# Seven block products instead of eight for five of the seven down-projection groups of an FFT-mixer and gated-MLP kernel, with products that accumulate on in their PSUM banks

## The chip, the cores and the metric

The kernel runs on one core of a Trainium2 chip. The metric is the device time of one execution in microseconds (us), taken as the median of repeated runs; lower is better. A core has a matrix engine (PE in the profile, with PEld for its weight loads), a vector engine (DVE), a scalar engine (ACT), a general engine (POOL), and SP, which here only issues DMAs. Matmuls write PSUM, of which a partition has eight banks of 512 float32. POOL touches only the on-chip memory SBUF; DVE and ACT read PSUM and SBUF.

## The reference

```python
# x: 1 x 2048 x 640;  w_gate, w_up: 640 x 1728;  w_down: 1728 x 640
def _A_ref(x, w_r, w_i):                      # filter in the 2-D Fourier domain
    X = jnp.fft.rfft2(x, axes=(-2, -1)) * (w_r + 1j * w_i)
    return jnp.fft.irfft2(X, s=(S, D), axes=(-2, -1))
def _B_ref(x, w_gate, w_up, w_down):
    g = jnp.einsum("bsd,df->bsf", x, w_gate)
    u = jnp.einsum("bsd,df->bsf", x, w_up)
    return jnp.einsum("bsf,fd->bsd", g * u, w_down)
h  = x + _A_ref(_layernorm(x), w_r, w_i)
h2 = h + _B_ref(_layernorm(h), w_gate, w_up, w_down)
```

## The kernel before, in words

The first 187 us or so are the Fourier filter, done as matmuls with cosine and sine tables, the second layer norm, and the start of the MLP. The rest is the MLP, and the change lies there.

The 2048 tokens form two blocks (`blk` 0 and 1) of eight tiles of 128 tokens; the first four tiles of a block are its half `sb` 0, the other four its half `sb` 1. The 1728 features form 14 chunks of 128 (the last has 64). Two chunks make a group `p`, whose rows of w_down are loaded together: group 6 (chunks 12 and 13) comes first in each block and is computed plainly, then groups 0 to 5 (chunks 0 to 11). In a group, the chunk `2p` is called even here and `2p+1` odd.

Every float32 operand of a matmul is split into a high part, rounded by ACT to the matmul's format, and a low part, the remainder, computed by DVE or POOL. A product then takes three matmuls: high·high, high·low, low·high.

For one chunk of a block, `strassen` computes gate and up of both halves as a 2x2 block matrix by Strassen's scheme: seven products `o1` to `o7` of 128x512 outputs, 54 matmuls of 512 columns in all, each product in a PSUM bank of its own (tile `e`). DVE adds them up with SBUF tiles `u2`, `u3`, `c22`, `p1` (lines 898 to 925), multiplies gate by up, ACT writes the high part of the result `h` (lines 911, 927) into `ht`, DVE the low part (lines 914, 930). The weights of the next chunk are prepared meanwhile in `prep`: ACT copies the high part of `stage` (the raw weights, a single buffer, filled by DMA in `load_raw`), POOL computes the low part (line 796), four block sums (799 to 802) and their low parts (812).

The down projection of a group runs while the next group's gate and up are computed: `down` takes one tile of 128 tokens, multiplies its `h` of two chunks by w_down (two halves of 320 columns, 12 matmuls in a `pair` of PSUM banks, tile `y`), and `acc` adds the 128x640 result to the residual `X[t]` in SBUF on DVE (line 601). The eight tiles are issued by `some` at fixed places inside `strassen`, all during the even chunk; the odd chunk has no down matmuls. One of the eight is held back at the end of a block (`defer`).

Nothing is reordered: the order of each engine's instructions is the order of the code. Each engine runs its own queue in order and waits on semaphores for others. The pool `work` (tag `wk`) hands out its buffers in turn; an allocation waits until the last reader of its buffer is done.

Of the kernel before, what the change touches and what calls it, by code (L numbers as in the profile page):

```python
# [16 lines left out]
P = 128  # L17
# [4 lines left out]
NC = 14  # L22
# [16 lines left out]
def f32(ap):  # L39
    return ap.bitcast(F32)  # L40
# [29 lines left out]
def tile_spectral_glu(ctx: ExitStack, tc: tile.TileContext, x, wf, wgu, wlast, wdown, wdlast,  # L70
# [4 lines left out]
    work = ctx.enter_context(tc.tile_pool(name="work", bufs=6))  # L75
# [14 lines left out]
    def bank(tag, bufs=2):  # L90
        return pools["y" if tag in ("im2", "ir2") else "a"].tile([P, 512], F32, tag=tag, name=tag, bufs=bufs)
# [4 lines left out]
    def single():  # L96
        return bank("e", 4)

    def wk(shape, name):
        return work.tile(shape, F32, tag="wk", name=name)  # L100
# [464 lines left out]
    def load_d(p):  # L565
        w = home("dA" if p in (0, 2, 4) else "dB", [P, 2, 1280], "wd", F32R)
        return split_in(("d", p), w, wdown[p] if p < 6 else wdlast, [wk([P, D], "draw") for _ in range(2)], nc.gpsimd)
# [106 lines left out]
    def t34(m):  # L674
        src = TJ["b"][:, :, 2 * m:2 * m + 2].rearrange("p j k n -> p k j n")
        hi, lo = ((t3[:, :, l] if m == 0 else xt[:, 1, 0:2, l]).rearrange("p k (j n) -> p k j n", j=4)
                  for l in range(2))
        return [lambda: act(hi, src, AF.Copy), lambda: tt(lo, src, f32(hi), op=OP.subtract)]
# [58 lines left out]
    def gate_parts(c, sb, slot, mid=()):  # L737
        pg, pu = PG[c, sb][0:2]
        u = wk([P, 512], "u")
        hh, hl = hts[:, slot, sb, 0], hts[:, slot, sb, 1]  # L740
# [12 lines left out]
    late = None  # L753
    for t in range(NT):
        for k in tside[t]:
            turn_mm(k)
        if t + 2 < NT:
            unfold(t + 2, dside[t], tside[t])
        else:
            for k in tside[t]:  # L760
                turn_hi(k)
                turn_lo(k)
        if t + 3 < NT:
            id_mm(t + 3)
        for f in aside[t]:
            f()
        if t == NT - 3:
            is1_mm(t)
            ht = home("qm", [P, 8192], "ht", F32R)
            hts, t3 = cut(ht, 0, 3, 2, 2, 512), cut(ht, 6144, 2, 2, 512)  # L770
            banks("a", "pglu")
            gu(NC - 1, 0)
        else:
            is1_mm(t)
        acc(t, PY[t], total[:, t:t + 1] if t < 8 else None)
        if t == NT - 2:
            late = gate_parts(NC - 1, 0, 0)
# [49 lines left out]
    def down(blk, p, slots, j, last=False, defer=False):  # L827
        t = blk * 8 + j
        sb, i = divmod(j, 4)
        ps = pair("y")  # L830
        w = W["d", p].rearrange("p l (c d) -> p l c d", c=2)
        seq = []
        for ci in range(2):
            hh, hl = (hts[:, slots[ci], sb, l, i * P:(i + 1) * P] for l in range(2))
            seq += [(hh, w[:, 0, ci]), (hh, w[:, 1, ci])]
            if 2 * p + ci < NC - 1:
                seq.append((hl, w[:, 0, ci]))

        def half(o, b):
            for n, (l, r) in enumerate(seq):  # L840
                mmx(o, l, r[:, 320 * b:320 * b + 320], n == 0, n == len(seq) - 1)

        if last and blk == 1 and j == 7:
            for b in range(2):
                o = (ps if b == 0 else pair("y"))[:, 0, 0:320]
                xv, ov = X[t][:, 320 * b:320 * b + 320], rows(out, t)[:, 320 * b:320 * b + 320]
                half(o, b)
                tt(xv, o, xv, op=OP.add)
                (nc.sync, nc.scalar)[b].dma_start(ov, xv)
            return  # L850
        for n, (l, r) in enumerate(seq):
            for b in range(2):
                mmx(ps[:, b, 0:320], l, r[:, 320 * b:320 * b + 320], n == 0, n == len(seq) - 1)
        if defer:
            return lambda: acc(t, ps)
        acc(t, ps)
        if last:
            nc.sync.dma_start(rows(out, t), X[t])

# [5 lines left out]
    def strassen(c, blk, slot, ahead, downs, side):  # L865
        wa, ws = W[c]

        def some(n):
            for _ in range(n):
                if downs:  # L870
                    downs.pop(0)()
                    if c:
                        pop(1)

        def at(n):
            for f in side.get(n, ()):
                f()
# [5 lines left out]
        hh, hl = ([hts[:, slot, sb, l] for sb in range(2)] for l in range(2))  # L883

        def product(w, a, ms, extra=()):
            o = single()
            triple(o, [(w, a + P * i, m) for i, m in enumerate(ms)] + list(extra))
            return o

        o1 = product(wa, 384, b11)  # L890
        p1, u2 = wk([P, 512], "p1"), wk([P, 512], "u2")
        act(p1, o1, AF.Copy)
        o6 = product(ws, 0, t2)
        at(0)
# [3 lines left out]
        tt(u2, o6, p1, op=OP.add)  # L898
        at(1)
        o7 = product(ws, 640, [(t3[:, k, 0], t3[:, k, 1]) for k in range(2)])  # L900
        u3, c22 = wk([P, 512], "u3"), wk([P, 512], "c22")
        tt(u3, u2, o7, op=OP.subtract)
        o5 = product(ws, 256, t1, [(wa, 896, b5[1])])
        tt(u2, o5, u2, op=OP.add)  # L904
        tt(c22, o5, u3, op=OP.add)
        some(2)
        at(2)
        o3 = product(ws, 896, b22, [(ws, 512, b5[1])])
        tt(o3, o3, u2, op=OP.add)  # L909
        tt(o3, o3, c22, op=OP.mult)  # L910
        act(hh[1], o3, AF.Copy)  # L911
        at(3)
        some(1)
        tt(hl[1], o3, f32(hh[1]), op=OP.subtract)
        some(1)
        o2 = product(wa, 0, b21, [(wa, 256, b5[0])])
        if ahead:
            ahead[2]()
            ahead[3]()
        tt(p1, o2, p1, op=OP.add)  # L920
        o4 = product(wa, 640, t4, [(wa, 896, b5[0])])
        some(1)
        at(6)
        tt(o4, o4, u3, op=OP.add)
        tt(o4, o4, p1, op=OP.mult)  # L925
        at(7)
        act(hh[0], o4, AF.Copy)  # L927
        at(4)
        some(2)
        tt(hl[0], o4, f32(hh[0]), op=OP.subtract)  # L930
        some(8)
        at(5)
# [3 lines left out]
    count = 0  # L936
    prev = None
    for n, (blk, p) in enumerate(steps):
        if p == 6:
            s13, s12 = count % 3, (count + 1) % 3  # L940
            if blk == 0:
# [14 lines left out]
                late = gate_parts(NC - 2, 0, s12)  # L956
# [4 lines left out]
                late = gate_parts(NC - 1, 1, s13)  # L961
# [8 lines left out]
            else:  # L970
# [17 lines left out]
                down(*prev, js[7], True)  # L988
                gu(NC - 1, 0)
                gate_parts(NC - 1, 0, s13)()  # L990
# [3 lines left out]
                late = gate_parts(NC - 2, 0, s12)  # L994
# [4 lines left out]
                gu(NC - 1, 1)  # L999
                for j in range(4):  # L1000
                    t1s[j][1]()
                wdn = load_d(p)
                late = gate_parts(NC - 1, 1, s13)
# [5 lines left out]
            gate_parts(NC - 2, 1, s12, wdn[0] if blk == 0 else ())()  # L1009
            for f in t34(1):  # L1010
                f()
            issue(wdn, (0, 1) if blk else (1,))
            prev = (blk, 6, (s12, s13))
            count += 2
# [4 lines left out]
            continue  # L1019
        wdn = load_d(p)  # L1020
        downs = [lambda j=j, prev=prev: down(*prev, j) for j in range(8)]
        slots = (count % 3, (count + 1) % 3)
        held = []
        if p == 5:
            downs.pop(3)
        for ci in range(2):
            c = 2 * p + ci
            side = {}
            ahead = None
            if c < 11:  # L1030
                ahead = prep(c + 1, blk)
                side[5] = [lambda c=c: load_raw(c + 2)] if c < 10 else []
            if ci == 0:
                side[3] = [lambda wdn=wdn: issue(wdn)]
            if c == 11 and blk == 0:
                pop(len(fill))
                dj = load_direct(1, [wk([P, D], "draw"), stage[:, 0:640], stage[:, 640:1280]])
                side[1] = [lambda: issue(dj[0]), lambda: issue(dj[1]), lambda: load_raw(0)]
# [7 lines left out]
                side[2] = [lambda: low(range(8))]  # L1046
            if c == 11:
                side[6] = [lambda prev=prev: held.append(down(*prev, 3, defer=True))]
                if blk == 0:
                    side[6] = [lambda: turn_mm(8)] + side[6] + [lambda: turn_hi(8)]  # L1050
                side[7] = [lambda: held[0]()]
            strassen(c, blk, slots[ci], ahead, downs if ci == 0 else [], side)
            count += 1
        prev = (blk, p, slots)
# [133 lines left out]
```

## Time and profile before

| what | value |
|---|---|
| time, median of 3 runs | 707.08 us (706.98 to 707.14) |
| profiled execution: first to last instruction (span) | 705.1 us |
| PE busy | 695.0 us, 3904 instructions |
| DVE busy | 459.3 us |
| ACT busy | 256.4 us |
| POOL busy | 281.6 us |
| granted clock of PE | 1.000 |
| bytes moved by DMA | 55.06 MB, mean 78 GB/s |

Busy times of the engines overlap. The profiled execution is one run of the same program; its span stands 1.98 us below the median of the timed runs, which also hold what lies before its first and behind its last instruction. A line of the profile such as `L106 PE MATMUL y<-wd,ht` names the code line, engine, operation, the tile written and the tiles read. Line 106 is the helper `mmx`, through which nearly all matmuls go, so groups are told apart by their tiles: `e<-...,wst` is gate and up, `y<-wd,ht` the down projection.

### The profile page before, as it was taken

To read this page: it belongs to the slowest core of one execution; us is meant where nothing else is said; L and a number is where in the kernel's file an instruction comes from. 1 tells how busy PE (TensorE), PEld (TensorE's weight loads), DVE (VectorE), ACT (ScalarE), POOL (GpSimd) and SP (SyncE) were. 2 spreads that over 40 slices of the span, in tenths; PEclk is the share of its full clock that TensorE was granted. 3 is DMA by queue.
4 is the path that set the end of the run, shared out by engine and by line. 5 is a ranking of instruction groups with operands and counts; after the bars stand their busy time and mean duration, and the time that the engine had idled before them with its cause. 6 is when DMAs were issued, how large, how long until landed. Compare 5 with 4: busy or idle time off the path is not lost.

```text
span 705.1 us, 10121 instructions
## 1 busy us (share of the span) xinstructions
PE 695.0 (99%) x3904; PEld 619.7 (88%) x3904; DVE 459.3 (65%) x807; ACT 256.4 (36%) x497; POOL 281.6 (40%) x260
## 2 busy tenths in 40 slices
PE   8999999999999999999999999999999999999998
PEld 8989998887798988888898989888888989898987
DVE  7968886998865566565655557565545555555464
ACT  6976664485522222131222273442212222322210
POOL 3101114321264645454535524074545454464600
PEclk9999999999999999999999999999999999999999
DMA  9426762001310102121212113301212121210103
GB/s 334 185 80 197 231 216 87 1 1 39 112 38 31 53 29 75 38 76 37 75 39 75 56 39 150 112 0 38 75 38 75 39 75 38 74 39 11 64 1 150
DMA packets 21073, 55.06 MB, mean 78 GB/s; under 512 B 2336, under 2 KB 7200, under 8 KB 21024
## 3 DMA queue, kind: packets, MB, share of 16 engines
q1 hardware_dynamic: 20304, 52.53, 21.4%
q0 software_dynamic: 288, 1.48, 0.6%
q8 instruction: 31, 0.51, 0.3%
q10 hardware_dynamic: 432, 0.39, 0.2%
q14 instruction: 18, 0.15, 0.1%
HBM read 49.16 MB, written 5.24 MB: 77 GB/s over the span
## 4 chain that ended last, share of the span: by engine, by line
PE 87%; DVE 7%; DMA 2%; issue 1%; ACT 1%; POOL 1%; SPq 0%; ACTq 0%; DVEq 0%
PE e L106 47%; PE y L106 26%; PE re L106 2%; PE im L106 2%; PE u L410 2%; DMA x<-in_x_dram 2%; PE im L452 2%; PE eo L106 2%; PE im L238 1%; PE ir L452 1%; DVE x L601 1%; DVE x L603 1%; DVE q L586 1%; DVE xt L648 1%; DVE q L587 1%
## 5 line engine op out<-in xcount | busy, mean ns | idle before, releaser
L106 PE MATMUL e<-xt,wst 128*128 128x512 f32 x864 | 206.8, 390 | 0.0
L106 PE MATMUL y<-wd,ht 128*128 128x320 f32 x1312 | 201.5, 310 | 0.6 <-DVE x L601 0.5
L106 PEld LDWEIGHTS y<-wd,ht 128*128 128x128 f32 x1312 | 195.3, 188 | 4.8 <-DVE x L601 1.7
L106 PEld LDWEIGHTS e<-xt,wst 128*128 128x128 f32 x864 | 160.7, 188 | 31.7
L601 DVE TENSOR_TENSOR x<-y,x 128x640 f32<-128x640 f32 x119 | 97.7, 822 | 69.9 <-PE y L106 69.4
L796 POOL TENSOR_TENSOR wst<-raw,wst 128x1024 fp32r<-128x1024 f32 x23 | 55.6, 2416 | 153.5 <-ACT wst L795 138.9
L812 POOL TENSOR_TENSOR wst<-raw,wst 128x896 fp32r<-128x896 f32 (+1 forms) x46 | 65.0, 1436 | 22.3 <-ACT wst L807 22.3
L557 POOL TENSOR_TENSOR wd<-draw,wd 128x640 fp32r<-128x640 f32 x28 | 44.9, 1629 | 71.8 <-ACT wd L556 71.8
L106 PE MATMUL e<-t,wst 128*128 128x512 f32 x288 | 73.2, 389 | 0.0
L911 ACT ACTIVATE ht<-e 128x512 fp32r<-128x512 f32 x24 | 14.4, 599 | 154.0 <-DVE e L910 154.0
L106 PEld LDWEIGHTS e<-t,wst 128*128 128x128 f32 x288 | 54.0, 188 | 11.7 <-DVE ht L747 0.5
L927 ACT ACTIVATE ht<-e 128x512 fp32r<-128x512 f32 x24 | 14.4, 599 | 111.8 <-DVE e L925 108.0
L106 PE MATMUL e<-xt,wdir 128*128 128x512 f32 x180 | 42.1, 393 | 0.2 <-DVE ht L751 0.2
L106 PEld LDWEIGHTS e<-xt,wdir 128*128 128x128 f32 x180 | 33.5, 188 | 7.6 <-issue 0.6
L795 ACT ACTIVATE wst<-raw 128x1024 fp32r<-128x1024 f32 x24 | 25.4, 1057 | 31.1 <-DMA raw<-in_wgu_dram 31.1
L106 PE MATMUL e<-ht,wst 128*128 128x512 f32 x144 | 36.5, 389 | 0.0
L904 DVE TENSOR_TENSOR u<-e,u 128x512 f32<-128x512 f32 x24 | 16.6, 692 | 29.5 <-PE e L106 29.4
L481 POOL CAST qr<-bits 1x128 fp32r<-1x128 f32 x15 | 4.2, 282 | 71.3 <-DVE qr L485 71.3
L106 PEld LDWEIGHTS e<-ht,wst 128*128 128x128 f32 x144 | 27.0, 188 | 5.6
L898 DVE TENSOR_TENSOR u<-e,p 128x512 f32<-128x512 f32 x24 | 16.6, 691 | 22.6 <-PE e L106 22.1
L909 DVE TENSOR_TENSOR e<-e,u 128x512 f32<-128x512 f32 x24 | 16.8, 700 | 22.0 <-PE e L106 22.0
L807 ACT ACTIVATE wst<-raw 128x896 fp32r<-128x896 f32 (+1 forms) x48 | 30.0, 675 | 3.2 <-POOL raw L801 2.4
(188 smaller groups left out, 1026.1 us busy)
## 6 DMA issues: line engine op xcount, KB each, us to landing
raw<-in_wgu_dram SPq DMA_DIRECT2D x24, 640.0 KB, 3.8
wts<-in_wf_dram SPq DMA_DIRECT2D x16, 644.0 KB, 3.9
draw<-in_wdown_dram SPq DMA_DIRECT2D x24, 320.0 KB, 4.4
x<-in_x_dram SPq DMA_DIRECT2D x15, 320.5 KB, 6.2
out_dram<-x SPq DMA_DIRECT2D x15, 320.0 KB, 2.2
bits<-in_mm_dram SPq DMA_DIRECT2D x32, 128.0 KB, 3.8
raw<-in_wgu_dram SPq DMA_DIRECT2D x4, 320.0 KB, 4.2
draw<-in_wdlast_dram SPq DMA_DIRECT2D x4, 320.0 KB, 2.8
```

Source lines behind the costliest of these rows:

```text
L106: nc.tensor.matmul(o, l, r, start=start, stop=stop, skip_group_check=True)
L452: nc.tensor.matmul(out, y[:, h, a:b], inv(g, h), start=n == 0, stop=n == len(ys) - 1)
L557: los.append(lambda r=r, a=a, b=b: engine.tensor_tensor(w[:, 1, a:b], r, f32(w[:, 0, a:b]), op=OP.subtract))
L601: tt(xv, ps[:, :, 0:320], xv, op=OP.add)
L795: act(wa[:, 0], stage[:, 0:1024], AF.Copy)
L796: ptt(wa[:, 1], stage[:, 0:1024], f32(wa[:, 0]), op=OP.subtract)
L807: act(ws[:, 0, o:o + b - a], stage[:, a:b], AF.Copy)
L812: ptt(ws[:, 1, o:o + b - a], stage[:, a:b], f32(ws[:, 0, o:o + b - a]), op=OP.subtract)
L898: tt(u2, o6, p1, op=OP.add)
L904: tt(u2, o5, u2, op=OP.add)
L909: tt(o3, o3, u2, op=OP.add)
L911: act(hh[1], o3, AF.Copy)
```

## The change

Down projection. For groups 0 to 4 the two halves `sb` of the tokens, the two chunks and the two column halves of w_down form a 2x2 block product, and `down_products` computes it with seven products of three matmuls (128x320) for each of four tile indices `j`: 84 matmuls a group in place of 96. The products are `p1` to `p7`. Their left operands are `h` parts and differences of them, kept as high and low parts in seven places of `ht` (`hop`): DVE computes the differences (lines 995, 996, 1018) and one of them is computed by POOL (line 1014, `s3`), ACT and DVE or POOL split them (`split`, lines 938 and 939). Their right operands are parts of w_down and differences, computed by DVE (`sums` in `load_d`) and split by ACT and POOL (lines 580, 581) into `wd` and a new tile `wt`. A product isn't kept apart: `p1`, `p6`, `p7`, `p4` of one `j` accumulate in one bank, `p5`, `p3` in another, which `p2` then begins anew (tile `d`, one bank each, four banks), and after each product DVE adds the bank as it then stands to one half of one `X[t]` (128x320, line 921). So a product that accumulates must wait for DVE's read of its bank. These are issued in batches of two or three products at places 2 to 7 of the even chunk and 1 to 4 of the odd chunk.

Groups 5 and 6 are computed by `down` as before, in two banks `d` and with two adds of 128x320.

Gate and up. The seven products are the same in number, but `strassen` accumulates: two banks `oa` and `ob` are read in between (by ACT into `h0`, `c22`, `h1`; by DVE in lines 988 and 991) and accumulated further. Gate times up is then one SBUF tile by another (line 992) for one half, PSUM by SBUF (1010) for the other. A sign moves into `t34(0)`.

Also: the pool `work` has 8 buffers in place of 6; `ahead[2]`, `ahead[3]` (the prepared weight sums) and w_down's preparation take other places; the two `h` of an odd chunk whose operands come last (`late`) are split at the start of the next chunk; at the end of a block the deferred tile goes; the scratch for DMA descriptors is set to 1024 bytes.

```diff
-    work = ctx.enter_context(tc.tile_pool(name="work", bufs=6))
+    work = ctx.enter_context(tc.tile_pool(name="work", bufs=8))
...
+        def sums():
+            tt(r[:, 0:320], r[:, 320:640], r[:, 0:320], op=sub)
+            tt(r[:, 320:640], q[:, 320:640], r[:, 320:640], op=sub)
+            tt(q[:, 320:640], q[:, 320:640], r[:, 0:320], op=sub)
+            tt(q[:, 0:320], q[:, 0:320], q[:, 320:640], op=sub)
...
+        def product(key, j):
+            a, which, n = DOWN[key]
...
+            l = [hop[:, a, k, j * P:(j + 1) * P] for k in range(2)]
+            first = key in ("p1", "p5", "p2")
+            mmx(o, l[0], r[0][:, n], first, False)
+            mmx(o, l[0], r[1][:, n], False, False)
+            mmx(o, l[1], r[0][:, n], False, True)
...
+            tt(xv, o, xv, op=OP.add)
...
+        order = [("p1", a), ("p5", a), ("p1", b), ("p5", b), ("p6", a), ("p3", a), ("p6", b), ("p3", b), ("p7", a),
+                 ("p2", a), ("p7", b), ("p2", b), ("p4", a), ("p4", b)]
...
+        oa = single()
+        product(oa, True, wa, 384, b11)
+        h0 = wk([P, 512], "h0")
+        act(h0, oa, AF.Copy)
+        for src, a in HELD.pop("late", ()):
+            split(src, a)
         if ahead:
             ahead[0]()
             ahead[1]()
-        tt(u2, o6, p1, op=OP.add)
         at(1)
...
+        product(ob, True, ws, 256, t1, [(wa, 896, b5[1])])
+        c22 = wk([P, 512], "c22")
+        act(c22, ob, AF.Copy)
         at(2)
...
+        product(oa, False, ws, 0, t2)
+        h1 = wk([P, 512], "h1")
+        act(h1, oa, AF.Copy)
         at(3)
...
+        product(ob, False, ws, 896, b22, [(ws, 512, b5[1])])
+        tt(h1, ob, h1, op=OP.add)
+        at(4)
+        product(oa, False, ws, 640, [(t3[:, k, 0], t3[:, k, 1]) for k in range(2)])
+        tt(c22, oa, c22, op=OP.add)
+        tt(h1, h1, c22, op=OP.mult)
+        if odd and p < 5:
+            a11, a21 = HELD["a11"], HELD["a21"]
+            tt(a21, a21, h1, op=OP.add)
+            tt(c22, a21, a11, op=OP.subtract)
+            for src, a in ((h1, 2), (a21, 3), (c22, 4)):
+                split(src, a)
...
+        oc = single()
+        product(oc, True, wa, 0, b21, [(wa, 256, b5[0])])
+        tt(h0, oc, h0, op=OP.add)
...
+        product(oa, False, wa, 640, t4, [(wa, 896, b5[0])])
+        tt(h0, oa, h0, op=OP.mult)
...
+        elif p < 5:
+            s4 = wk([P, 512], "s4")
+            tt(s4, h0, c22, op=OP.subtract)
+            HELD["late"] = [(s4, 6), (h0, 1)]
...
+                def rest(wdn=wdn, ahead=ahead):
+                    split(HELD["a11"], 0, nc.gpsimd)
+                    ahead[2]()
+                    ahead[3]()
+                    wdn[3]()
+                    split(HELD["s3"], 5, nc.gpsimd)
+                    wdn[4]()
+
+                side[4].append(rest)
```

Three places show how instructions move. First PE, from the end of an odd chunk through an even chunk of a group in the middle of block 0, before:

```order
L106 MATMUL e<-xt,wst 128x512 x3
L106 MATMUL y<-wd,ht 128x320 x24
L106 MATMUL e<-xt,wst 128x512 x9
L106 MATMUL y<-wd,ht 128x320 x24
L106 MATMUL e<-xt,wst 128x512 x18
L106 MATMUL y<-wd,ht 128x320 x48
```

The same place after (`wst`, `xt`, `t` and `ht` beside `e` are gate and up; `d` is the down projection):

```order
L109 MATMUL e<-xt,wst 128x512 x24
L109 MATMUL e<-t_1856,wst 128x512 x6
L109 MATMUL e<-xt,wst 128x512 x3
L109 MATMUL d<-wd,ht 128x320 x9
L109 MATMUL e<-t_1856,wst 128x512 x6
L109 MATMUL d<-wd,ht 128x320 x3
L109 MATMUL d<-wt,ht 128x320 x3
L109 MATMUL d<-wd,ht 128x320 x3
L109 MATMUL e<-xt,wst 128x512 x9
L109 MATMUL d<-wt,ht 128x320 x3
L109 MATMUL d<-wd,ht 128x320 x3
L109 MATMUL d<-wt,ht 128x320 x3
```

Three long runs of down matmuls a group have become ten batches of 6 or 9, threaded between products of gate and up.

Second DVE, the arithmetic of one odd chunk, before:

```order
L898 TENSOR_TENSOR u_3427<-e,p_3426 128x512
L902 TENSOR_TENSOR u_3451<-u_3427,e 128x512
L904 TENSOR_TENSOR u_3427<-e,u_3427 128x512
L905 TENSOR_TENSOR c_3452<-e,u_3451 128x512
L909 TENSOR_TENSOR e<-e,u_3427 128x512
L910 TENSOR_TENSOR e<-e,c_3452 128x512
L914 TENSOR_TENSOR ht<-e,ht 128x512
L920 TENSOR_TENSOR p_3426<-e,p_3426 128x512
L924 TENSOR_TENSOR e<-e,u_3451 128x512
L925 TENSOR_TENSOR e<-e,p_3426 128x512
L930 TENSOR_TENSOR ht<-e,ht 128x512
```

And after, from the second accumulated bank of an odd chunk to the two late splits, which stand in the next chunk:

```order
L991 TENSOR_TENSOR c_3495<-e,c_3495 128x512
L992 TENSOR_TENSOR h_3515<-h_3515,c_3495 128x512
L995 TENSOR_TENSOR h_3338<-h_3338,h_3515 128x512
L996 TENSOR_TENSOR c_3495<-h_3338,h_3291 128x512
L939 TENSOR_TENSOR ht<-h_3515,ht 128x512
L939 TENSOR_TENSOR ht<-h_3338,ht 128x512
L939 TENSOR_TENSOR ht<-c_3495,ht 128x512
L1004 TENSOR_TENSOR h_3463<-e,h_3463 128x512
L1010 TENSOR_TENSOR h_3463<-e,h_3463 128x512
L1018 TENSOR_TENSOR s_3597<-h_3463,c_3495 128x512
L939 TENSOR_TENSOR ht<-s_3597,ht 128x512
L939 TENSOR_TENSOR ht<-h_3463,ht 128x512
```

Before, each of these reads a PSUM bank (`e`) and at most one SBUF tile; after, nine of the twelve read two SBUF tiles.

Third POOL, one odd chunk, before:

```order
L796 TENSOR_TENSOR wst<-raw,wst 128x1024
L799 TENSOR_TENSOR raw<-raw 128x256
L800 TENSOR_TENSOR raw<-raw 128x384
L801 TENSOR_TENSOR raw<-raw 128x256
L802 TENSOR_TENSOR raw<-raw 128x256
L812 TENSOR_TENSOR wst<-raw,wst 128x896
L812 TENSOR_TENSOR wst<-raw,wst 128x256
```

And after:

```order
L835 TENSOR_TENSOR wst<-raw,wst 128x1024
L838 TENSOR_TENSOR raw<-raw 128x256
L839 TENSOR_TENSOR raw<-raw 128x384
L840 TENSOR_TENSOR raw<-raw 128x256
L841 TENSOR_TENSOR raw<-raw 128x256
L939 TENSOR_TENSOR ht<-h_4301,ht 128x512
L851 TENSOR_TENSOR wst<-raw,wst 128x896
L851 TENSOR_TENSOR wst<-raw,wst 128x256
L581 TENSOR_TENSOR wt<-draw,wt 128x640
L939 TENSOR_TENSOR ht<-c_4320,ht 128x512
L581 TENSOR_TENSOR wt<-draw,wt 128x320
```

POOL's work of the odd chunk has grown by two splits of `h` operands and two parts of `wt`, which stand behind the weight preparation.

More of the change, by code (lines that the diff above doesn't have):

```diff
@@ L97, in single, with lane @@
         return bank("e", 4)
+    def lane():
+        return pools["y"].tile([P, 512], F32, tag="d", name="d", bufs=4)
     def wk(shape, name):
@@ L677, in t34, with low @@
                   for l in range(2))
-        return [lambda: act(hi, src, AF.Copy), lambda: tt(lo, src, f32(hi), op=OP.subtract)]
+        if m:
+            return [lambda: act(hi, src, AF.Copy), lambda: tt(lo, src, f32(hi), op=OP.subtract)]
+        def low():
+            for k in range(2):
+                nc.vector.scalar_tensor_tensor(lo[:, k], src[:, k], -1.0, f32(hi[:, k]), op0=OP.mult, op1=OP.subtract)
+        return [lambda: act(hi, src, AF.Copy, scale=-1.0), low]
     def transp(t):
@@ L776, in tile_spectral_glu @@
         if t == NT - 2:
[L777 removed]
+            late = gate_parts(NC - 1, 0)
     transp(6)
@@ L825, in operand, with down @@
         return xt[:, sb, k, 0], xt[:, sb, k, 1]
-    def down(blk, p, slots, j, last=False, defer=False):
+    def down(blk, p, j, last=False):
         t = blk * 8 + j
         sb, i = divmod(j, 4)
-        ps = pair("y")
+        ps = [lane() for _ in range(2)]
         w = W["d", p].rearrange("p l (c d) -> p l c d", c=2)
@@ L863, in issue, with split, strassen @@
                 h()
-    def strassen(c, blk, slot, ahead, downs, side):
-        wa, ws = W[c]
[L868 to L873, printed above, removed]
-        def at(n):
+    HELD = {}
+    def split(src, a, engine=None):
+        hi, lo = (hop[:, a, l] for l in range(2))
+        act(hi, src, AF.Copy)
+        (engine or nc.vector).tensor_tensor(lo, src, f32(hi), op=OP.subtract)
+    def strassen(c, blk, ahead, downs, side):
+        wa, ws = W[c]
+        p, odd = divmod(c, 2)
+        def at(n):
+            if downs.get(n):
+                for f in downs[n]:
+                    f()
+                if c:
+                    pop(1)
             for f in side.get(n, ()):
@@ L882, in strassen, with product @@
         b5 = [operand(sb, 4) for sb in range(2)]
[L883 to L894, printed above, removed]
+        def product(o, first, w, a, ms, extra=()):
+            terms = [(w, a + P * i, m) for i, m in enumerate(ms)] + list(extra)
+            n = len(terms)
+            for i, (w, a, m) in enumerate(terms):
+                whi, wlo = w[:, 0, a:a + P], w[:, 1, a:a + P]
+                mmx(o, whi, m[0], first and i == 0, False)
+                mmx(o, whi, m[1], False, False)
+                mmx(o, wlo, m[0], False, i == n - 1)
+        oa = single()
[4 more added lines that the diff above has]
+            split(src, a)
         if ahead:
@@ L897, in strassen @@
             ahead[1]()
-        tt(u2, o6, p1, op=OP.add)
         at(1)
[L900 to L906, printed above, removed]
+        ob = single()
+        product(ob, True, ws, 256, t1, [(wa, 896, b5[1])])
+        c22 = wk([P, 512], "c22")
@@ new lines, in strassen @@
+        tt(h1, ob, h1, op=OP.add)
[9 more added lines that the diff above has]
+                split(src, a)
+        elif odd:
+            split(h1, 4)
@@ L918, in strassen @@
+        at(5)
+        oc = single()
+        product(oc, True, wa, 0, b21, [(wa, 256, b5[0])])
+        tt(h0, oc, h0, op=OP.add)
+        if ahead and not odd:
             ahead[2]()
             ahead[3]()
-        tt(p1, o2, p1, op=OP.add)
-        o4 = product(wa, 640, t4, [(wa, 896, b5[0])])
-        some(1)
         at(6)
-        tt(o4, o4, u3, op=OP.add)
-        tt(o4, o4, p1, op=OP.mult)
-        at(7)
[L927 to L930, printed above, removed]
@@ L931, in strassen @@
-        some(8)
-        at(5)
+        product(oa, False, wa, 640, t4, [(wa, 896, b5[0])])
+        tt(h0, oa, h0, op=OP.mult)
+        if not odd:
+            HELD["a11"], HELD["a21"] = h0, h1
+            if p < 5:
+                nc.gpsimd.tensor_tensor(c22, h0, h1, op=OP.subtract)
+                HELD["s3"] = c22
+        elif p < 5:
+            s4 = wk([P, 512], "s4")
+            tt(s4, h0, c22, op=OP.subtract)
+            HELD["late"] = [(s4, 6), (h0, 1)]
+        at(7)
+        if c == 11:
+            split(h0, 5)
@@ L1044, in low @@
                         normalise(8 + k, TJ["z"][:, k] if k < 6 else wk([P, D], "z"))
[L1046 to L1054, printed above, removed]
+                side[4].append(lambda: low(range(8)))
+                side[7] += [lambda: turn_mm(8), lambda: turn_hi(8)]
+            strassen(c, blk, ahead, slots[ci], side)
+        prev = (blk, p)
     for j in (4, 5, 6, 0, 1, 2, 3, 7):
```

127 lines of the change are left out of this document (83 added, 44 removed).

## The prediction

> **What bounds the kernel now.** I read the page's engine totals and its clock row first:
>
> ```profile
> PE 695.0 (99%) x3904; PEld 619.7 (88%) x3904; DVE 459.3 (65%) x807; ACT 256.4 (36%) x497; POOL 281.6 (40%) x260
> PEclk9999999999999999999999999999999999999999
> ```
>
> PE is busy for 695.0 of 705.1 us and never throttled: time falls only if PE has fewer matmuls or each comes sooner, and rises wherever PE has to wait. Since a busy PE may hide waits, I next read the timeline of PE through one group in mid-kernel (start, length, matmuls of a run), and the busy times of that window:
>
> ```profile
> 321.32 7.32 PE L106 MATMUL y<-wd,ht 128*128 128x320 f32 x48
> ...
> 346.87 3.68 PE L106 MATMUL y<-wd,ht 128*128 128x320 f32 x24
> 350.38 2.23 PE L106 MATMUL e<-xt,wst 128*128 128x512 f32 x9
> 352.45 3.68 PE L106 MATMUL y<-wd,ht 128*128 128x320 f32 x24
> 355.96 4.27 PE L106 MATMUL e<-xt,wst 128*128 128x512 f32 x18
> 360.07 7.20 PE L106 MATMUL y<-wd,ht 128*128 128x320 f32 x48
> 367.10 1.55 PE L106 MATMUL e<-xt,wst 128*128 128x512 f32 x6
> 368.49 1.52 PE L106 MATMUL e<-t,wst 128*128 128x512 f32 x6
> 369.85 1.52 PE L106 MATMUL e<-ht,wst 128*128 128x512 f32 x6
> ...
> 360.07:398.69 38.62, 38.62 (x206) 34.34 (x204) 21.50 (x34) 9.04 (x14) 20.00 (x17) 1.00 0.18 60
> ```
>
> From start to start, 24 down matmuls take 352.45 to 355.96, 3.51 us, and 48 take 7.03: 146.5 ns each. Six of gate and up take 1.36 (368.49 to 369.85): 226.7 ns each. A group is then 108 x 226.7 + 96 x 146.5 = 24.48 + 14.06 = 38.54 us, and the window says 38.62: PE waits for nothing, and what is left is a switch. The nine `e` behind a down run take 2.07, not 2.04, and the six at 367.10 take 1.39, not 1.36: 0.03 us each time PE comes back from the down projection, three times a group. DVE (21.50), ACT (9.04) and POOL (20.00) have room in 38.62.
>
> **The change: what PE sheds.** Each of five groups in two blocks goes from 96 to 84 down matmuls: 120 x 146.5 ns = 17.6 us, all on the path. Gate and up keep 54 matmuls a chunk. The returns from down to gate and up rise from 3 to 10 a group: 70 x 0.03 = 2.1 us back (none if the price belongs to a long run; 4 if accumulating waits double it). The Trainium skill (TensorE: Matmul & The Clock Gate, Back-to-back issue gap) gives N/2.4 + 2.5 ns a matmul, so 135.8 ns here and 16.3 us for the 120; the trace disagrees with its 146.5, and decides.
>
> Without waits the span would be 705.1 - 17.6 + 2.1 = 689.6 us. The timed runs stand 1.98 above the profiled span, so 691.6.
>
> **What is added beside PE.** Prices:
>
> ```profile
> L601 DVE TENSOR_TENSOR x<-y,x 128x640 f32<-128x640 f32 x119 | 97.7, 822 | 69.9 <-PE y L106 69.4
> 700.69 0.49 DVE L848 TENSOR_TENSOR x<-y,x 128x320 f32<-128x320 f32 x1
> L914 DVE TENSOR_TENSOR ht<-e,ht 128x512 fp32r<-128x512 f32 x24 | 16.4, 684 | 10.3 <-ACT ht L911 10.3
> 336.87 0.70 DVE L909 TENSOR_TENSOR e<-e,u 128x512 f32<-128x512 f32 x1 [0.75 <-PE e L106]
> 337.60 0.70 DVE L910 TENSOR_TENSOR e<-e,c 128x512 f32<-128x512 f32 x1
> 347.07 0.69 DVE L904 TENSOR_TENSOR u<-e,u 128x512 f32<-128x512 f32 x1 [1.35 <-PE e L106]
> 347.68 0.68 DVE L905 TENSOR_TENSOR c<-e,u 128x512 f32<-128x512 f32 x1
> L892 ACT ACTIVATE p<-e 128x512 f32<-128x512 f32 x24 | 14.3, 596 | 41.0 <-PE e L106 41.0
> L795 ACT ACTIVATE wst<-raw 128x1024 fp32r<-128x1024 f32 x24 | 25.4, 1057 | 31.1 <-DMA raw<-in_wgu_dram 31.1
> L557 POOL TENSOR_TENSOR wd<-draw,wd 128x640 fp32r<-128x640 f32 x28 | 44.9, 1629 | 71.8 <-ACT wd L556 71.8
> L796 POOL TENSOR_TENSOR wst<-raw,wst 128x1024 fp32r<-128x1024 f32 x23 | 55.6, 2416 | 153.5 <-ACT wst L795 138.9
> L812 POOL TENSOR_TENSOR wst<-raw,wst 128x896 fp32r<-128x896 f32 x23 | 48.9, 2128 | 22.3 <-ACT wst L807 22.3
> L800 POOL TENSOR_TENSOR raw<-raw 128x384 f32<-128x384 f32 x23 | 23.4, 1016 | 1.8
> L812 POOL TENSOR_TENSOR wst<-raw,wst 128x256 fp32r<-128x256 f32 x23 | 17.1, 744 | 0.0
> L799 POOL TENSOR_TENSOR raw<-raw 128x256 f32<-128x256 f32 x23 | 17.0, 740 | 1.8
> ```
>
> DVE, a group: before 22 x 0.68 + 8 x 0.82 = 21.5, as the window says; after, 18 of 512 columns, 28 adds of 320 at 0.49 and 4 weight sums at 0.49: 12.2 + 13.7 + 2.0 = 27.9 us of the 37.1 that PE then needs. POOL: w_down goes from 1280 to 2240 columns (960/640 x 1.63 = 2.4) and three 512-column operations come, 1.3 each by the 640 row: 20.0 + 6.3 = 26.3. ACT rises to some 15. All fit, so these totals cost nothing; only order can.
>
> I walk the tightest chain, the end of an odd chunk. Products of 6 and 9 matmuls take 1.36 and 2.04, batches 1.32 or 0.88. From the chunk's start PE ends its fifth product (`t3`) at 13.0, the next at 15.04, the last at 17.08. DVE reads the accumulated bank (line 991) from 13.2, 1.8 us ahead of the last product, which accumulates on it. Dependent instructions start 0.73 apart (336.87, 337.60), independent ones 0.61: lines 992, 995, 996 start at 13.9, 14.7, 15.4, three splits to 17.8, 1004 and 1010 to 19.2, 1018 ends at 19.9. In the next chunk (zero at 17.08) ACT makes two high parts of 0.6 behind that, from 2.9 to 4.0; DVE's low parts end at 4.8; the add of the first `p1` at 5.2. PE needs that add at 6.5, when `p6` accumulates in its bank: 1.3 us spare. ACT, behind the two high parts, copies weights (1.06) and then the bank for `c22`, done at 5.5; PE accumulates on that bank at 7.4: 1.9 spare. The weight DMA that ACT waits for (31.1 us in the L795 row) has by then long been issued; the buffer is freed by POOL at about 12.8 of the odd chunk. On POOL, the parts of `wt` finish at 16.5, more than 6 us before `p6` needs them. So the cover is 1.3 us.
>
> **What may use up the cover.** Before, each DVE instruction of a chunk read PSUM and one SBUF tile; 14 a group now read two SBUF tiles. Elsewhere the trace shows such instructions beside POOL:
>
> ```profile
> 126.58 1.06 POOL L590 TENSOR_TENSOR yt<-q 128x318 f32<-128x318 f32 x1 [1.85 <-DVE m L178]
> 126.95 1.37 DVE L557 TENSOR_TENSOR wdir<-raw,wdir 128x640 fp32r<-128x640 f32 x1
> ...
> 188.76 1.23 DVE L678 TENSOR_TENSOR ht<-bt,ht 128x1024 fp32r<-128x1024 f32 x1
> 192.21 1.82 DVE L678 TENSOR_TENSOR xt<-bt,xt 128x1024 fp32r<-128x1024 f32 x1 [0.25 <-ACT xt L678]
> 188.96 3.98 POOL L557 TENSOR_TENSOR wd<-draw,wd 128x640 fp32r<-128x640 f32 x2 [25.41 <-ACT wd L556]
> ...
> 460.87 3.53 POOL L557 TENSOR_TENSOR wd<-draw,wd 128x640 fp32r<-128x640 f32 x2 [25.75 <-ACT wd L556]
> 460.20 1.23 DVE L678 TENSOR_TENSOR xt<-bt,xt 128x1024 fp32r<-128x1024 f32 x1 [0.25 <-ACT xt L678]
> ```
>
> The DVE subtraction of 640 columns takes 1.37 us begun in the midst of a POOL instruction, where the 640-column add takes 0.82: 0.55 more for 0.69 of overlap. The 1024 columns at 192.21 take 1.82, without POOL 1.23. Where DVE began first (188.76, 460.20) it kept 1.23, and POOL's pair took 3.98 and 3.53 for about 3.2. The later one pays half to four fifths of the overlap. The Trainium skill (SBUF — State Buffer, Who interferes with whom) speaks against the change here: a DVE instruction with two SBUF inputs contends with POOL's reads, and the pair of ports is an exclusive lock; these rows agree in kind.
>
> In the odd chunk's tail POOL runs two `wt` parts and a split, 12.8 to 16.5, beside lines 992, 995 and 996: I take +0.35, +0.75 and +0.5, 1.6 us on the chain, against 1.3 spare. PE then waits 0.3 us a group (0 without contention, 1.0 if the later one is blocked throughout). This holds for eight of the ten groups: 2.4 us. In group 0 the odd chunk has no down matmuls (group 6 is done in its even chunk) and lasts only 12.2 us, while POOL has 13.6 us of work in it: the low part of the weights 2.4, four sums 3.2, a split 1.3, the sums' low parts 2.9, then `wt` 1.6, a split 1.3, `wt` 0.9. DVE meets POOL at every step, six times about 0.5, 3 us; I take 1.0 us of waiting at each of two such places (0 to 2.9): 2.0 us. The ends of the blocks I take at nothing: ACT's eight normalisations lie beside the same matmuls as before.
>
> Sum: 689.6 + 2.4 + 2.0 = 694.0, and 1.98 for the timed run: **696.0 us**.
>
> **Rivals.**
> *Contention costs PE nothing.* The cover of 1.3 us is more than I think, as DVE often starts first. For it: both cases where DVE began first show it undisturbed. Then 691.6, or 689.5 if the switches are free too. Chance 0.24.
>
> *The later one is blocked to the end.* That is the exclusive lock taken literally (SBUF — State Buffer, as above). Then 8 x 1.0 + 2 x 2.9 = 13.8 us of waits: 705.4. Against it: 0.36 us paid for 0.55 of overlap at 460.87. Chance 0.14, of which 0.04 within 0.2% of before; 0.2% is about what a measurement of this kernel can tell from no change.
>
> *DVE becomes the bound, slower.* The 14 instructions with two SBUF inputs all meet POOL and pay 0.8 each, the most that one row shows (POOL at 188.96, 3.98 for 3.2): 27.9 + 11.2 = 39.1 us a group against 38.6 before, ten times: 707.1 + 5 = 712. It decides from (38.6 - 27.9)/14 = 0.76 us each. In block 0 the layer-norm statistics, threaded between, add some 5 us in three groups. Against it: POOL is idle a quarter of the time, and the adds from PSUM aren't touched. Chance 0.10.
>
> **How the numbers follow.** My forecast, waits between 1 and 8 us, has 0.52; its time is 696.0. The range 690 to 703 holds it, most of the first rival and the mild part of the second. Faster by over 0.2%: 0.52 + 0.24 + 0.10 = 0.86; within: 0.04; slower: 0.10.
>
> **What would show it.** In the trace after: 1192 down matmuls into `d` in place of 1312 into `y`; runs of nine at 1.32 us; a middle group of 37.1 to 37.6 us in place of 38.62; PE's waits (in rows of PE or PEld) released by DVE L921, a few tenths each, in even chunks before `p6`, larger in the first even chunk behind group 0; DVE lines 992, 995, 996, 939 above 0.70 us on average, 1.0 or so where POOL is busy; DVE some 520 to 560 us busy, POOL about 345. Wrong it would be if a middle group takes 38 us or more, if PE waits for lines 988 or 991, or if 939 stays at 0.69.

## The result and the profile after

The changed kernel took 717.48 us (median of four runs, 714.97 to 717.91) against 707.03 us (706.74 to 707.14) for the kernel before in the same session: a ratio of 1.0142 [1.0126, 1.0158]. It is 1.4% slower. The forecast was 696.0 us, in a range of 690 to 703.

The page of the changed kernel, its engine totals, its clock row and the shares of the chain that ended last:

```profile
PE 687.9 (96%) x3784; PEld 606.2 (85%) x3784; DVE 539.5 (75%) x1022; ACT 312.1 (44%) x605; POOL 363.2 (51%) x322
PEclk9999999999999999999999999999799999999999
PE 69%; DVE 25%; ACT 3%; issue 2%; POOL 1%; DVEq 0%; ACTq 0%
```

PE has the 120 instructions less that were announced, but its busy time fell only from 695.0 to 687.9 us, and it now idles for 28 us of a span of 716.0. A quarter of the chain lies on DVE. The clock row, which gives the granted clock of PE in tenths of full speed, has a dip. The groups of instructions by line (the last column is idle time before them) show which DVE instructions grew; in the kernel before, DVE's work on 512 columns, with one operand in PSUM, took 0.68 to 0.70 us:

```profile
L992 DVE TENSOR_TENSOR h<-h,c 128x512 f32<-128x512 f32 x24 | 35.5, 1479 | 0.8
L995 DVE TENSOR_TENSOR h<-h,h 128x512 f32<-128x512 f32 x10 | 17.7, 1767 | 1.0
L996 DVE TENSOR_TENSOR c<-h,h 128x512 f32<-128x512 f32 x10 | 12.3, 1227 | 0.3
```

The waits of PE, largest first (us in total, times, longest):

```profile
PE d L109 <- DVE x L921: 13.6, 12, 3.2
PE d L109 <- DVE ht L939: 3.6, 2, 1.8
```

To see where they lie I cut the span into groups, always at the same matmul of the even chunk, except the first row, which runs from the start of group 0 to the start of group 1. Busy times by window (from:to, length, PE, PEld, DVE, ACT, POOL, granted clock and DMA), for group 0, 1 and 2 of block 0 and group 1 of block 1:

```profile
187.76:225.79 38.03, 36.89 (x190) 31.99 (x188) 23.16 (x36) 15.15 (x26) 26.01 (x20) 1.00 0.15 53
227.31:271.87 44.56, 39.38 (x193) 33.80 (x193) 36.65 (x62) 14.87 (x26) 32.82 (x26) 0.96 0.21 65
271.87:310.12 38.25, 37.33 (x194) 32.56 (x193) 31.91 (x61) 14.07 (x25) 27.58 (x22) 1.00 0.16 52
502.13:547.25 45.12, 41.15 (x194) 35.36 (x193) 32.85 (x52) 14.87 (x26) 32.76 (x26) 0.89 0.21 65
```

A middle group takes 38.25 us where 37.1 to 37.6 was forecast, and the group behind group 0 takes 44.56 and 45.12. In PE's timeline these are the places: the steady wait first, then group 1 of block 0, then group 1 of block 1.

```profile
277.97 0.70 PE L109 MATMUL d<-wt,ht 128*128 128x320 f32 x3 [0.92 <-DVE x L921]
...
278.98 2.23 PE L109 MATMUL e<-xt,wst 128*128 128x512 f32 x9
281.04 0.60 PE L109 MATMUL d<-wt,ht 128*128 128x320 f32 x3
...
231.87 0.85 PE L109 MATMUL d<-wd,ht 128*128 128x320 f32 x4 [1.79 <-DVE ht L939]
232.55 1.55 PE L109 MATMUL e<-t,wst 128*128 128x512 f32 x6
...
237.73 0.71 PE L109 MATMUL d<-wt,ht 128*128 128x320 f32 x3 [3.19 <-DVE x L921]
...
239.03 3.51 PE L109 MATMUL e<-xt,wst 128*128 128x512 f32 x9
...
506.68 0.85 PE L109 MATMUL d<-wd,ht 128*128 128x320 f32 x4 [1.78 <-DVE ht L939]
507.37 2.19 PE L109 MATMUL e<-t,wst 128*128 128x512 f32 x6
509.36 1.00 PE L109 MATMUL d<-wd,ht 128*128 128x320 f32 x3
512.55 1.17 PE L109 MATMUL d<-wt,ht 128*128 128x320 f32 x3 [2.19 <-DVE x L921]
...
514.31 4.04 PE L109 MATMUL e<-xt,wst 128*128 128x512 f32 x9
```

Every middle group stops about 0.9 us ahead of the first `p6`, for DVE's add of `p1`. Behind group 0 PE stops twice, first for a split (line 939) and then for an add (line 921), and after that the same nine matmuls take 3.51 and 4.04 us instead of 2.23: the matrix engine itself has become slow for a while.

What DVE was doing then is in the timeline of DVE and of POOL at the end of a middle group's odd chunk (start, length):

```profile
305.45 1.47 DVE L992 TENSOR_TENSOR h<-h,c 128x512 f32<-128x512 f32 x1
307.02 1.60 DVE L995 TENSOR_TENSOR h<-h,h 128x512 f32<-128x512 f32 x1
308.65 1.26 DVE L996 TENSOR_TENSOR c<-h,h 128x512 f32<-128x512 f32 x1
...
304.79 1.59 POOL L581 TENSOR_TENSOR wt<-draw,wt 128x640 fp32r<-128x640 f32 x1
306.32 1.75 POOL L939 TENSOR_TENSOR ht<-c,ht 128x512 fp32r<-128x512 f32 x1
308.03 1.33 POOL L581 TENSOR_TENSOR wt<-draw,wt 128x320 fp32r<-128x320 f32 x1
```

Add starts and lengths: POOL ends at 306.38, 308.07 and 309.36, and DVE ends 0.54, 0.55 and 0.55 us behind each. The two engines take turns. By these times DVE's instruction starts while POOL's is running and gets nowhere until that has ended; POOL's next one starts meanwhile and is held in the same way (1.75 us where an undisturbed one takes 1.30); by then DVE's next is behind it again. The three instructions cost 1.47 + 1.60 + 1.26 - 3 x 0.69 = 2.26 us more than undisturbed ones.

### The profile page after: what moved, and what is told of

Same layout as the page of the kernel before. It is cut to its first block, busy times and chain, and to the rows that moved or that the text cites. A ratio compares the mean times of both kernels' runs of the same rounds, so it can differ in the third digit from the quotient of the medians.

```text
span 716.0 us, 10313 instructions
## 1 busy us (share of the span) xinstructions
PE 687.9 (96%) x3784; PEld 606.2 (85%) x3784; DVE 539.5 (75%) x1022; ACT 312.1 (44%) x605; POOL 363.2 (51%) x322
## 4 chain that ended last, share of the span: by engine, by line
PE 69%; DVE 25%; ACT 3%; issue 2%; POOL 1%; DVEq 0%; ACTq 0%
PE e L109 32%; PE d L109 21%; DVE ht L939 5%; DVE h L995 2%; DVE h L992 2%; PE re L109 2%; PE im L109 2%; PE u L413 2%; PE im L455 2%; PE eo L109 2%; DVE c L996 2%; PE im L241 1%; PE re L282 1%; DVE c L991 1%; DVE h L1010 1%
## 5 line engine op out<-in xcount | busy, mean ns | idle before, releaser
L109 PE MATMUL d<-wd,ht 128*128 128x320 f32 x832 | 147.7, 312 | 4.7 <-DVE ht L939 3.6
L921 DVE TENSOR_TENSOR x<-d,x 128x320 f32<-128x320 f32 x280 | 123.9, 483 | 37.6 <-PE d L109 33.4
L109 PEld LDWEIGHTS d<-wd,ht 128*128 128x128 f32 x832 | 131.6, 189 | 13.9 <-DVE ht L939 4.1
L109 PE MATMUL d<-wt,ht 128*128 128x320 f32 x360 | 70.8, 314 | 13.0 <-DVE x L921 13.0
L109 PEld LDWEIGHTS d<-wt,ht 128*128 128x128 f32 x360 | 57.9, 189 | 17.8 <-DVE x L921 16.0
L988 DVE TENSOR_TENSOR h<-e,h 128x512 f32<-128x512 f32 x24 | 16.6, 691 | 43.3 <-PE e L109 38.5
L938 ACT ACTIVATE ht<-h 128x512 fp32r<-128x512 f32 x48 | 29.8, 625 | 34.1 <-DVE h L992 19.0
L580 ACT ACTIVATE wd<-draw 128x320 fp32r<-128x320 f32 (+1 forms) x30 | 15.7, 558 | 66.2 <-DVE draw L588 66.2
L896 DVE TENSOR_TENSOR x<-d,x 128x320 f32<-128x320 f32 x62 | 27.3, 484 | 13.3 <-PE d L109 13.3
L992 DVE TENSOR_TENSOR h<-h,c 128x512 f32<-128x512 f32 x24 | 35.5, 1479 | 0.8
L560 POOL TENSOR_TENSOR wd<-draw,wd 128x640 fp32r<-128x640 f32 x8 | 14.7, 1858 | 42.0 <-ACT wd L559 42.0
```

The lines of the kernel that those rows point to most:

```text
L109: nc.tensor.matmul(o, l, r, start=start, stop=stop, skip_group_check=True)
L560: los.append(lambda r=r, a=a, b=b: engine.tensor_tensor(w[:, 1, a:b], r, f32(w[:, 0, a:b]), op=OP.subtract))
L580: act(o[:, 0, a:a + n], src, AF.Copy)
L896: tt(xv, ps[b][:, 0:320], xv, op=OP.add)
L988: tt(h1, ob, h1, op=OP.add)
L992: tt(h1, h1, c22, op=OP.mult)
```

## The experiments

Theory: a DVE instruction with two SBUF inputs that meets a POOL instruction gets nowhere until POOL's has ended, and PE's stops follow from that. Rivals: the accumulation in gate and up costs PE time whatever the operands; the order of the down products, which leaves the odd chunk of group 0 short, is the cause; POOL's work itself is late for PE.

**One input from PSUM.** The sum of line 988 stays in its PSUM bank, the product of line 992 too in odd chunks, and lines 995 and 996 take it from there. The number and order of each engine's instructions stay, and so do the results. Line 996 now subtracts POOL's earlier difference `s3`, so it no longer needs the result of line 995.

```diff
-        tt(h1, ob, h1, op=OP.add)
+        tt(ob, ob, h1, op=OP.add)
...
-        tt(h1, h1, c22, op=OP.mult)
+        tt(ob if odd else h1, ob, c22, op=OP.mult)
...
-            tt(a21, a21, h1, op=OP.add)
-            tt(c22, a21, a11, op=OP.subtract)
+            tt(a21, ob, a21, op=OP.add)
+            tt(c22, ob, HELD["s3"], op=OP.subtract)
```

> Change: in the odd chunk the sum and the product for one half stay in PSUM (written in place in the bank), and the difference is taken from POOL's earlier one, so that lines 992, 995, 996 and the first split each read one SBUF tile and PSUM; same number of DVE instructions in the same order, same POOL work. Theory A (DVE instructions with two SBUF inputs are held by POOL's): these three instructions fall from 1.48, 1.68 and 1.24 us to 0.7, the waits of about 1 us before p6 in the steady groups go, those behind group 0 shrink to 1 to 2 us a place, the clock stays at 1.000; 696 to 704 us. Theory B (the DVE queue is simply too long behind the odd chunk, whatever POOL does): the waits stay, 714 to 718 us.

It took 696.22 us (695.83 to 696.48), 0.9849 [0.9832, 0.9865] of the kernel before: 21.3 us less than the change, for a few moved operands. Its groups by line:

```profile
L992 DVE TENSOR_TENSOR e<-e,c 128x512 f32<-128x512 f32 x12 | 8.4, 699 | 0.4
L995 DVE TENSOR_TENSOR h<-e,h 128x512 f32<-128x512 f32 x10 | 6.9, 692 | 1.0
L996 DVE TENSOR_TENSOR c<-e,c 128x512 f32<-128x512 f32 x10 | 6.8, 681 | 0.0
```

Its groups 1 and 2 by window:

```profile
227.12:266.13 39.01, 37.56 (x194) 32.57 (x193) 31.01 (x62) 14.02 (x24) 30.18 (x25) 1.00 0.25 84
266.13:303.13 37.00, 37.00 (x194) 32.55 (x193) 28.80 (x61) 14.17 (x24) 26.32 (x22) 1.00 0.16 54
```

POOL does the same work beside them, and the three are back at 0.69 us. The middle group is free of waits at 37.00 us. The group behind group 0 falls from 44.56 to 39.01, with the clock at 1.00. What is left there is mostly another mechanism, in the timeline of PE and ACT:

```profile
231.71 1.66 PE L109 MATMUL e<-t,wst 128*128 128x512 f32 x6 [1.23 <-ACT h L971]
...
231.06 0.60 ACT L971 ACTIVATE h<-e 128x512 f32<-128x512 f32 x1 [4.85 <-POOL wt L581]
```

ACT cannot copy the first bank until POOL, late with the work of the short chunk, has read the raw w_down for the last time. Both are tiles of the pool `work`, so the copy most likely takes over that buffer; this was not tested by itself. The group is 2.0 us longer than the middle one, in both blocks.

**A longer odd chunk in group 0.** Group 6's eight plain tiles are split between the two chunks of group 0, four and four, in place of all in the even one. The operands are those of the change.

```diff
-            slots[0] = {n: [lambda j=j, prev=prev: down(*prev, j) for j in k] for n, k in enumerate(js, 2)}
+            for ci in range(2):
+                slots[ci] = {n: [lambda j=j, prev=prev: down(*prev, j)]
+                             for j, n in zip(range(4 * ci, 4 * ci + 4), range(2 - ci, 6))}
```

> Change: the eight down tiles of group 6 are spread over both chunks of group 0, four and four, in place of all in the even chunk; the odd chunk of group 0 gets as long as the others. Theory A (POOL's 13.6 us of work does not fit the short odd chunk of group 0, and DVE meets it at every step): the group behind group 0 falls from 44.6 and 42.4 to about 38.3 us, the clock there returns to 1.000, and 703 to 707 us in all. Theory B (group 1 waits for something of its own, its first use of the Strassen operands): no change there, 715 to 718 us.

It took 704.54 us (704.19 to 704.86), 0.9967 [0.9954, 0.998] of before and 12.9 us less than the change. Group 1 of block 0 by window:

```profile
226.95:265.45 38.50, 37.29 (x194) 32.56 (x193) 32.17 (x61) 14.34 (x25) 27.58 (x22) 1.00 0.17 53
```

At 38.50 us the group behind group 0 is now nearly like the middle ones of the change (38.25), and like them it still has its wait of about 1 us ahead of `p6`; the clock holds. So the short chunk multiplies the damage in two places, and the turn-taking alone sets the rest.

**POOL's reads taken away.** In the odd chunks of groups 0 to 4 the five low parts that POOL computes there (of the prepared weight sums, of `wt`, of two operands) are left out, and POOL writes zeros instead. DVE keeps its two SBUF inputs.

```diff
+        if engine is not None and QUIET:
+            engine.memset(f32(lo), 0.0)
+            return
         (engine or nc.vector).tensor_tensor(lo, src, f32(hi), op=OP.subtract)
```

> Leaves out low parts: the five low parts that POOL computes in the odd chunk of groups 0 to 4 behind the weight sums become writes of zeros, so POOL reads nothing beside DVE's chain there. Theory A (DVE is held by POOL's reads): lines 992, 995, 996 take 0.7 us, no waits before p6, 690 to 694 us. Theory C (POOL's writes hold DVE too): they stay above 1 us in part, 700 to 712. Theory B (queue too long): waits stay, 712 to 718 us.

It took 692.18 us (691.98 to 692.59), 0.9792 [0.9778, 0.9807], with a span of 690.1 us. Lines 995 and 996 are 1005 and 1006 in this kernel; its groups by line:

```profile
L1005 DVE TENSOR_TENSOR h<-h,h 128x512 f32<-128x512 f32 x10 | 6.9, 692 | 1.4 <-DVE h L1002 0.5
L1006 DVE TENSOR_TENSOR c<-h,h 128x512 f32<-128x512 f32 x10 | 6.9, 692 | 0.3
```

Groups 1 and 2 by window:

```profile
226.95:263.95 37.00, 37.00 (x194) 32.55 (x193) 29.81 (x61) 14.43 (x24) 21.97 (x22) 1.00 0.20 65
263.95:300.95 37.00, 37.00 (x194) 32.55 (x193) 29.28 (x60) 14.43 (x24) 21.95 (x22) 1.00 0.16 54
```

With the same operands on DVE but no POOL reads beside them the instructions are undisturbed. Together with the first experiment this shows the pair as the cause: either side removed, the cost is gone. The zeros are short and had ended when DVE's chain began, so POOL was idle beside it, and whether POOL's writes alone would hold DVE stays open. The product of line 992 (1002 here) still averages 0.97 us, since in the even chunks POOL was left as it is; PE waits for none of that.

**Gate and up alone.** Gate and up accumulate as in the change; all groups of the down projection are computed plainly, all eight tiles in the even chunk.

```diff
-        if p >= 5:
+        if p >= 0:
             return split_in(("d", p), w, wdown[p] if p < 6 else wdlast, raws, nc.gpsimd)
...
-            fs = down_products(*prev, (0, 1)) + down_products(*prev, (2, 3))
-            slots[0] = dict(zip(range(2, 8), fs))
-            slots[1] = dict(zip((1, 2, 3, 7 if p == 5 else 4), fs[6:]))
+        js = [[0], [1], [2], [3], [4, 5], [6, 7]]
+        slots[0] = {n: [lambda j=j, prev=prev: down(*prev, j) for j in k] for n, k in enumerate(js, 2)}
```

> One part alone: gate and up accumulate in their banks as in the change, while all groups' down projection is done by eight tiles of 12 matmuls as before (no Strassen operands, no differences, no extra POOL work). If accumulating gate and up costs PE nothing, 706 to 708 us as before; if PE waits in each chunk for the reads of lines 981 to 991, some 0.2 us a chunk or more, above 711 us.

It took 710.73 us (709.84 to 711.19), 1.0053 [1.0038, 1.0068]: between the cases expected, and slower than before by 3.9 us. A middle group by window, and PE's largest wait in the MLP in its timeline (line 988 of this kernel is ACT's copy of a bank):

```profile
306.22:344.93 38.71, 38.71 (x205) 34.25 (x205) 19.71 (x36) 11.21 (x18) 20.67 (x17) 1.00 0.15 52
```

```profile
274.20 2.33 PE L109 MATMUL e<-xt,wst 128*128 128x512 f32 x9 [0.82 <-ACT c L988]
```

The group is 0.09 longer than the 38.62 of before, what three more returns at the 0.03 of the forecast would cost. The rest are a few single waits: four for ACT's copies (0.70, 0.82, 0.51 and 0.26 us) and one for POOL (0.46). Accumulation alone gains nothing and loses 0.5%; it is no large cost either, so that rival falls. The product of line 992 (999 here) reads two SBUF tiles in this kernel too and takes 1.16 us on average, but none of PE's waits is for it.

**Both cures.** The first two edits together; everything is computed.

> Change: the chain of the odd chunk through PSUM and the spread of group 6's down tiles together; the output is the reference's. Theory A leaves no waits but those at the start of group 0 (0.5 and 0.7 us): the 1.2 us that ACT waits for a buffer which POOL still reads behind group 0 goes with the longer odd chunk. Span 690 to 691.5 us, 692 to 693.5 timed. If instead something else than POOL beside DVE makes group 1 wait, it stays near 696.

It took 692.2 us (691.99 to 692.83), 0.9795 [0.9782, 0.9808] of the kernel before, and 25.3 us less than the change. Its timeline shows lines 995 and 996 beside a POOL instruction that overlaps both, and its window of group 1:

```profile
297.86 0.69 DVE L995 TENSOR_TENSOR h<-e,h 128x512 f32<-128x512 f32 x1
298.47 0.68 DVE L996 TENSOR_TENSOR c<-e,c 128x512 f32<-128x512 f32 x1
...
297.80 1.30 POOL L939 TENSOR_TENSOR ht<-c,ht 128x512 fp32r<-128x512 f32 x1
```

```profile
227.73:264.73 37.00, 37.00 (x194) 32.55 (x193) 28.86 (x62) 14.16 (x24) 26.27 (x22) 1.00 0.16 55
```

Neither engine pays anything, and the group behind group 0 takes 37.00 us as well. POOL does all its work here, so the rival that this work is late for PE falls too. Against groups of 37.00 us the changed kernel lost some 1.25 in each of eight middle groups and 7.56 and 8.12 behind group 0, 25.7 us in all; the two spans, 716.0 and 690.9, differ by 25.1. The places named hold the whole loss. This is the version to keep: it beats both kernels.

## Why the prediction was wrong

**The work that PE sheds was right.** The forecast put the span without waits at 689.6 us: 17.6 us of matmuls saved, 2.1 back for the returns. With POOL's reads away the span was 690.1, with both cures 690.9, and a group took 37.00 where 37.1 was worked out. The 1192 matmuls into `d`, the price of a return (six matmuls behind a batch take 1.55 us, others 1.52) and line 921 as the releaser of PE's waits ahead of `p6`, larger behind group 0, came as said; the two waits for line 939, 3.6 us, were not named. POOL was busy for 363.2 us where some 345 was forecast, and for 346.3 with both cures: POOL pays for the meetings as well. DVE's total of 539.5 lies in the 520 to 560 named, but by luck: with both cures it is 501.5, and a group of block 1 then takes 25.7 us of DVE where 27.9 was worked out, so that two errors covered each other.

**The step that failed is the price of meeting POOL.** The forecast read "the later one pays half to four fifths of the overlap" and took 0.35, 0.75 and 0.5 us for lines 992, 995 and 996, 1.6 us against 1.3 of cover. Measured were 0.78, 0.91 and 0.57, 2.26 us, and 2.26 - 1.3 is close to the 0.9 us that PE now waits: the cover was right, the price was not. The rows quoted then already held the rule. POOL's instruction at 126.58 ended at 127.64 and DVE's 640 columns at 128.32, 0.68 later, where they take 0.82 alone; POOL's pair at 188.96 ended at 192.94 and DVE's 1024 columns at 194.03, 1.09 later, where they take 1.23; in the changed kernel it is 0.55 for 0.69. Each time 0.14 us of start is hidden, and the rest begins only when POOL has ended. Dividing the loss by the overlap made a share out of that fixed 0.14. And I priced the meetings singly: in a chain each DVE instruction meets the next POOL instruction, which its own predecessor has held back.

**Behind group 0 the same error was larger.** The timeline of DVE and POOL in group 0's odd chunk:

```profile
222.63 1.84 DVE L992 TENSOR_TENSOR h<-h,c 128x512 f32<-128x512 f32 x1
224.58 2.43 DVE L995 TENSOR_TENSOR h<-h,h 128x512 f32<-128x512 f32 x1
227.04 1.12 DVE L996 TENSOR_TENSOR c<-h,h 128x512 f32<-128x512 f32 x1
228.09 3.73 DVE L939 TENSOR_TENSOR ht<-h,ht 128x512 fp32r<-128x512 f32 x2
231.74 1.35 DVE L939 TENSOR_TENSOR ht<-c,ht 128x512 fp32r<-128x512 f32 x1
...
223.88 3.73 POOL L851 TENSOR_TENSOR wst<-raw,wst 128x896 fp32r<-128x896 f32 x2
227.58 2.02 POOL L581 TENSOR_TENSOR wt<-draw,wt 128x640 fp32r<-128x640 f32 x1
229.55 1.71 POOL L939 TENSOR_TENSOR ht<-c,ht 128x512 fp32r<-128x512 f32 x1
```

Six DVE instructions, which undisturbed take 3 x 0.69, 1.28 and 0.68, pay 3.32 + 2.45 + 0.67 = 6.4 us; I had taken 3, and from it 1.0 us of waiting, where 3 less the cover of 1.3 would have been 1.7. PE then waits 1.79 + 3.19 us, near 6.4 - 1.3, and 1.78 + 2.19 in block 1: 8.95 us in place of 2.0. In block 1 the second wait is 1.0 us shorter because PE comes to it as much later: its clock has already fallen, and the two runs before it take 2.19 and 1.00 us for 1.55 and 0.60.

**A term was missing: the clock.** After those waits the same number of matmuls kept PE busy for 39.38 and 41.15 us where 37.33 is usual: 5.9 us that no part of the forecast had.

**The sum.** From 694.0 to 716.0 there are 22.0 us: waits ahead of `p6` in eight groups 7.4 in place of 2.4 (the 13.6 of line 921, less the 3.19 and 2.19 behind group 0 and 0.8 elsewhere), 5.0; behind group 0, 7.0; the clock, 5.9; small waits at the starts of group 0 and the end of block 0, 2.0 (0.46, 0.68, 0.26 and 0.62), which I had put at nothing, less 0.5 that the kernel before lost there, 1.5; and what a stop costs beside its wait, 0.33 a group (PE is busy for 37.33 us in the middle group with a stop and for 37.00 in one without; the run at 277.97 takes 0.70 where the like run at 281.04 takes 0.60), 3.3 in ten groups. That makes 22.7; a group without stops took 37.00 in place of 37.1, which takes some 1.0 back and leaves 21.7.

**The rivals.** "The later one is blocked to the end" had the rule right, with a chance of 0.14. Its eight waits of 1.0 are nearly the measured 0.9; its 705.4 falls short because it took 2.9 for each group 0 and nothing for the clock. The Trainium skill (SBUF — State Buffer, Who interferes with whom) had said that a DVE instruction with two SBUF inputs contends with POOL's reads, and that one with at most one does not (outside two-port modes, which by the same section `tensor_tensor` lacks): the 1.60 and 0.69 us of line 995 agree with both sentences. I had given that rival little weight because 0.36 us were paid for 0.55 of overlap, which is a hidden start again, of 0.2 us on POOL. "DVE becomes the bound" fell: DVE is busy for 31.91 of the 38.25 us of a middle group. "Contention costs nothing" is what the cure of both gives, 692.2 against 691.6. I had called it wrong if a middle group took 38 us or more; it does.

## What to carry to other kernels

Beside a POOL that reads SBUF, count the SBUF inputs of each DVE instruction: here one input cost nothing (0.69 us beside POOL), and each instruction with two cost what was left of POOL's current one, less 0.14 us. On a chain that PE waits for, leave the running value in its PSUM bank; off such a chain the longer instructions made PE wait nowhere here (line 992 in even chunks). Price a chain of such instructions by turns, not by shares of overlap, and look for the shortest stage, where the other engine's work fills the whole time. A cover that runs out is paid twice where the clock of PE falls after its wait, 5.9 us here.

## What the runs showed of the hardware

Strict turns between DVE and POOL were not expected: both engines' instructions stretch (DVE's from 0.69 to 1.60 us, POOL's from 1.30 to 1.75). For 512 columns DVE's ends 0.55 us behind POOL's, and POOL's 1.15 us behind DVE's (308.07 against 306.92).

The granted clock fell after short stops. By window in the changed kernel, around the two waits of block 1, then after those of block 0 and right behind:

```profile
506.60:509.30 2.70, 2.62 (x10) 2.25 (x11) 2.60 (x4) 0.00 (x0) 0.77 (x1) 0.76 0.60 154
512.50:518.10 5.60, 5.55 (x15) 4.73 (x16) 2.17 (x5) 2.37 (x5) 5.29 (x5) 0.50 0.00 0
239.00:242.40 3.40, 3.40 (x11) 2.69 (x11) 1.54 (x4) 0.37 (x1) 3.17 (x4) 0.59 0.00 0
242.40:246.00 3.60, 3.60 (x23) 3.34 (x22) 3.07 (x6) 1.26 (x2) 3.52 (x5) 1.00 0.00 0
```

In block 1 it fell behind a single wait of 1.78 us: its mean is 0.76 over the next 2.7 us, and the slowing was there before the second wait began, as the three matmuls at 509.36 take 1.00 us where 0.60 is usual. Behind the second wait it stood at 0.50. In block 0 the six matmuls behind a like wait of 1.79 still took 1.55 us, against 2.19 in block 1, and it fell only behind the next wait, of 3.19. With waits of 0.9 to 1.2 us (the second experiment) it stayed at 1.00. The Trainium skill (TensorE: Matmul & The Clock Gate, Why this matters for your kernels) puts the limit at idle gaps of about 3 us; the 3.19 of block 0 agrees, the 1.78 of block 1 does not, and the measurement decides. What makes the two blocks differ was not tried. The executions differ as well: in the one of 714.97 us the mean granted clock was 0.994, in the other three 0.990.
